# GQA attention fused with a squared-ReLU feed-forward: the third batch's loads get new end times in the kernel's event model, and scores wait per turned part

## The chip, the cores and the metric

The kernel runs on one core of a Trainium2 chip. The metric is the device time of one execution in microseconds (us); the figure for a kernel is the median of its runs. The engines are named as in the profile: PE is TensorE (PEld its weight loads), DVE is VectorE, ACT is ScalarE, POOL is GpSimd, SP is the sync engine, which here only issues DMAs.

## The reference, cut to what matters

```python
# q (8, 16, 384, 64), k and v (8, 4, 384, 64); each k/v head serves 4 q heads
scores = 0.125 * q @ k.T              # per head, 384 x 384
attn = softmax(scores)                # over the last axis
x = (attn @ v) -> (3072, 1024)        # batch and sequence by heads and head_dim
h = maximum(x @ w_in, 0)              # w_in (1024, 2048)
out = (h * h) @ w_out                 # w_out (2048, 1024), out (3072, 1024) float32
```

There are 8 batches of 384 tokens. A batch has 8 pairs of heads; pairs are numbered through, p = 0 to 63, so pair 16 is the first of batch 2, the third batch.

## The kernel before, in words

**Who does what.** For each pair, PE computes transposed scores from qT and kT (L514), ACT exponentiates them (L519), PE multiplies with v (L534), and DVE divides by the row sums into o_sb (L542, L544). The result is turned into xT, the feed-forward's input: by a DMA transpose on SP (put_x, L434), or for batch 1 by PE (row_turn, L571) and a DVE copy (L575). The feed-forward of a batch has 16 up tiles (row_up, PE L625): DVE applies the ReLU into one of three hr buffers (L636) and ACT squares hr into h2T (L644); for batch 0 every second tile is squared by POOL instead (L641). The down projection of batch 0 and of a part of batch 1 is plain (row_down, L683); the others take seven products for eight (L791), with sums made by DVE (L699).

**How inputs of a batch arrive.** POOL issues the loads of k, q and v (load_k L208, load_q L220, load_v L214), which also cast to bf16. There is one buffer of each for all batches from 1 on (k_st, q_next, v_st). POOL then copies k twice into k_dup (dup_all_k, L355), SP issues six DMA transposes (PARTS: two of k, L361, four of q, L369), and POOL copies v into v_aug (prepare_v, L383). load_third issues the loads of batch 2 and the second half of w_out behind them, as soon as the turns of batch 1 have freed q_next. The loads of later batches are issued by load_next when the second pair of the batch before them has been put.

**What sets the order.** A planner in Python writes out each engine's instructions in one fixed order. `Recorder.add` keeps a clock of its own: each operation gets a start and an end from the ends of what it depends on and from estimated durations (for a load 0.9 us on the queue and 12 us, LOADS, to landing; for a DMA transpose 1.25 and 2.2 us). `at(time, fn)` puts an action at a time of that clock. On the chip the engines follow the order, and wait on semaphores for what is really late; so a wrong estimate doesn't break the result, but an instruction can stand at the head of its queue and hold what is behind it. The clock is set to START, 30.0 us, after a hand-written beginning.

The main loop at the end picks the next work of PE among attention steps and feed-forward tiles, whichever can begin first. Attention is paced: each feed-forward piece adds its time over PACE of the present batch to a credit, and an attention step is due when the credit reaches the step's share. An attention step may be chosen only when its condition holds. For row_scores that is, before the change:

```python
return [piece(i) for i in range(3)], over, lambda: before in exped and p // NPB in prepared
```

`prepared` holds batches; batch b enters it when its sixth part has been issued. For batch 2 the order of attention is: attend of pair 15, both halves of the scores of pair 16, then on. The row-wise pieces use half of PE's rows each, so two of them run beside each other.

ready_at(b) places the preparation of a batch: at the time when k, v and q have all landed by the clock, it issues the k copy, the first part and the v copy, and then a part every 1.3 us.

Of the kernel before, what the change touches and what calls it, by code (L numbers as in the profile page):

```python
# [136 lines left out]
def bass_gqa_attention__then__ffn_squared_relu_kernel(  # L137
# [66 lines left out]
    sc_flat = sc_ps.ap().rearrange("p b c -> p (b c)")  # L204


    def load_k(b, after=()):
        R.add("gpsimd", lambda g: g.dma_start(  # L208
            k_st.ap().rearrange("p g j d -> p g (j d)"),
            k[b].rearrange("g (p j) d -> p g (j d)", j=NJ)),  # L210
            writes=["k_st"], dma="k", after=after, ns=900.0, lat=LOADS)

    def load_v(b, after=()):
        R.add("gpsimd", lambda g: g.dma_start(  # L214
            v_st.ap().rearrange("p g j d -> p g (j d)"),
            v[b].rearrange("g (p j) d -> p g (j d)", j=NJ)),
            writes=["v_st"], dma="v", after=after, ns=900.0, lat=LOADS)

    def load_q(b, after=()):
        R.add("gpsimd", lambda g: g.dma_start(  # L220
            q_st[1], q[b].rearrange("h (p j) d -> p h (j d)", j=NJ)),
            writes=[("q_st", 1, c) for c in range(NPB)], dma="q", after=after, ns=900.0, lat=LOADS)

    NWB = 8
    WC = FF // NWB
# [151 lines left out]
    def prepare(b, parts=range(6)):  # L377
        for i in parts:
            turn, x = PARTS[i]
            turn(b, x)  # L380
# [64 lines left out]
    def now():  # L445
        return R.idle_at["tensor"]
# [55 lines left out]
        return free.pop(0)  # L502

    exped, scaled = set(), {NPB - 1}
    turned, usable, upped = {}, {0}, set()

    def row_scores(p, half):
        kt, qt, keys, k_keys = operands(p)

        def piece(i):  # L510
            u = 3 * half + i
            j, x = u // 2, u % 2
            rows = ROWS[x]
            return Piece(x, 162.5, lambda pe: pe.matmul(sc_ps[:, i, 0:S], kt[rows, j * 128:(j + 1) * 128], qt[rows, :]),  # L514
                         keys + k_keys[j:j + 1], [("sc", i)])

        def over(last):
            def exp():
                R.add("scalar", lambda e: e.activation(expT[p % NEX][:, 3 * half:3 * half + 3, :], sc_ps[:, 0:3, 0:S],  # L519
                                                       AF.Exp, scale=0.125), ns=1130.0,  # L520
                      reads=[("sc", i) for i in range(3)], writes=[("expT", p % NEX, 3 * half + i) for i in range(3)])
                exped.add((p, half))

            at(R.ops[last]["end"], exp)

        before = (p, 0) if half else (p - 1, 1)
        return [piece(i) for i in range(3)], over, lambda: before in exped and p // NPB in prepared

    def row_attend(p, then=None):
        b, g = p // NPB, (p % NPB) // 2  # L530

        def piece(r, f, j):
            rows = ROWS[r]
            return Piece(r, 33.0, lambda pe: pe.matmul(  # L534
                po_v[:, f % NJ, f // NJ, :], expT[p % NEX][rows, 2 * j + f % 2, f // 2 * 128:f // 2 * 128 + 128],
                v_aug[b % 2][rows, g * NJ + j, :], start=(r == 0 and f == 0 and j == 0), stop=(r == 1),
                skip_group_check=True),
                [("expT", p % NEX, 2 * j + f % 2), ("v_aug", b % 2), ("v_one", b % 2)], ["po"])

        def done():  # L540
            rinv_v = rinv[p % 2].ap().unsqueeze(3)
            R.add("vector", lambda e: e.reciprocal(rinv_v, po_v[:, :, :, D:D + 1]),  # L542
                  reads=["po"], writes=[("rinv", p % 2)], ns=200.0)
            op = R.add("vector", lambda e: e.tensor_tensor(o_sb[p % NO][:, :, :, :], po_v[:, :, :, 0:D],  # L544
                                                           rinv_v.to_broadcast([128, NJ, 2, D]), ALU.mult),
                       reads=["po", ("rinv", p % 2)], writes=[("o_sb", p % NO, x) for x in range(2)], ns=560.0)
            scaled.add(p)
            assert b - NXT in upped or b < NXT
            if b == 1:
                at(R.ops[op]["end"], lambda: o_turns.append(p))  # L550
                return
            landed = put_x(p)
            turned[b] = turned.get(b, 0) + 1
            if turned[b] == NPB:
                usable.add(b)
            if then:
                then(landed)

        lo, hi = ([piece(r, f, j) for f in range(2 * NJ) for j in range(NJ)] for r in range(2))
        return lo, lambda last: hold_back(hi, last, done), lambda: p - 1 in scaled and ((p, 1) in exped)  # L560

    F_TURN = [sc_bf[:, 3, 0:S], sc_bf[:, 4, 0:S]] + [t.ap().bitcast(bf16)[:, 0:S] for t in f_ps]

# [18 lines left out]
    q_turns, o_turns = [], []  # L582

    def load_third():
        for load in (load_k, load_q, load_v):
            load(2)
        load_w_out(1)
        ready_at(2)

    def next_turn():  # L590
        if q_turns and (len(free) > 1 or not o_turns):
            c = q_turns.pop(0)

            def then():
                if c == NPB - 1:
                    prepared.add(1)
                    load_third()

            return row_turn(q_st[1][:, 2 * c:2 * c + 2, :].rearrange("p h e -> p (h e)"), [("q_st", 1, c)],
                            qT[1][:, c], [("qT", 1, c)], then)  # L600
        p = o_turns.pop(0)

        def then():
            turned[1] = turned.get(1, 0) + 1
            if turned[1] == NPB:
                usable.add(1)

        return row_turn(o_sb[p % NO].ap().rearrange("p i s d -> p (i s d)"), [("o_sb", p % NO, x) for x in range(2)],
                        xT[1][:, p % NPB], [("xT", 1, p % NPB)], then)
# [8 lines left out]
    def row_up(b, c, then=None, final=False):  # L618
        i = yield from next_bank()
        acc, key = F_BANKS[i]  # L620
        r = tiles[0] = (tiles[0] + 1) % NHR

        def piece(h, kc):
            rows = ROWS[h]
            return Piece(h, 162.5, lambda pe: pe.matmul(acc[:, 0:S], w_in_sb[rows, kc, c * 128:(c + 1) * 128],  # L625
                                                        xT[b % NXT][rows, kc, :], start=(h == 0 and kc == 0),
                                                        stop=(h == 1 and kc == NKC - 1), skip_group_check=True),
                         [("w_in", c * 128 // WC), ("xT", b % NXT, kc)], [key])

        def done():  # L630
            if r in hr_open:
                at(now() + 100.0, done)
                return
            hr_open.add(r)
            free.append(i)
            op = R.add("vector", lambda e: e.tensor_scalar_max(hr[r][:, :], acc[:, 0:S], 0.0),  # L636
                       reads=[key], writes=[("hr", r)], ns=560.0)

            def square():
                if b == 0 and c % 2:  # L640
                    op = R.add("gpsimd", lambda e: e.tensor_tensor(h2T[b % 2][:, c, :], hr[r][:, :], hr[r][:, :], ALU.mult),  # L641
                               reads=[("hr", r)], writes=h2(b, c), ns=830.0)
                else:
                    op = R.add("scalar", lambda e: e.activation(h2T[b % 2][:, c, :], hr[r][:, :], AF.Square),  # L644
                               reads=[("hr", r)], writes=h2(b, c), ns=520.0)
                squared.add((b, c))
                hr_open.discard(r)
                if then:
                    at(R.ops[op]["end"], then)

            at(R.ops[op]["end"], square)
            if final:
                upped.add(b)

        lo, hi = ([piece(h, kc) for kc in range(NKC)] for h in range(2))
        yield from push("up", lo, hi, done)
# [346 lines left out]
            yield from wait(lambda: b in usable)  # L1003
            yield from feed_forward(b)

    PACE = {1: (2300.0, 2300.0), 2: (4300.0, 3500.0), 3: (4500.0, 3600.0), 4: (6300.0, 4400.0), 5: (5800.0, 3800.0), **{b: (5800.0, 3800.0) for b in range(6, B + 1)}}
    LONE = 6000.0

    turns = [lambda banks=RING, g=g: first_kT(g, 1, banks) for g in range(HKV)]
# [44 lines left out]
    up_step(0, 0, 6, 8)  # L1054
    q_turns.extend(range(NPB - len(turns), NPB))
    exped.update(((NPB, 0), (NPB, 1)))
    prepared = {1}

    for o in R.ops:
        if o["dma"] is None or o["end"] < START:  # L1060
# [5 lines left out]
    def ready_at(b):  # L1066

        def part(i):
            prepare(b, (i,))
            if i < 5:  # L1070
                at(now() + 1300.0, lambda: part(i + 1))
            else:
                prepared.add(b)

        def begin():
            dup_all_k(b, "gpsimd")
            part(0)
            prepare_v(b)

        t = max(R.ready("gpsimd", ["k_st", "v_st"], []), R.ready("sync", [("q_st", 1, 0)], []))  # L1080
        at(t, begin)

    def load_next(b):
        def then(landed):
# [108 lines left out]
```

## Time and profile before

| | us |
|---|---|
| median of 5 runs | 426.71 |
| lowest and highest | 426.28, 427.42 |
| the profiled execution | 426.28 |
| its span, first to last instruction | 424.5 |
| busy: PE, PEld | 409.0, 314.2 |
| busy: DVE, ACT, POOL | 216.9, 215.0, 55.4 |
| mean granted PE clock | 0.992 |

How to read what follows. The page cuts the span into 40 slices of 10.6 us; a digit is the busy share in tenths, and PEclk is the clock that PE was granted. A window row gives for a stretch (from:to in us from the span's start) its length and, for PE, PEld, DVE, ACT and POOL in this order, the busy time and the instructions in brackets, then the granted clock, the share of the DMA engines' time and GB/s. A row of waits says which engine, at which line, waited for what: us in total, times, longest. A timeline row gives start, duration, engine, line, operation, what is written and read, and in square brackets the idle time before it and its releaser. A row of DMA queues has packets, MB, and the time that packets took as a share of 16 engines.

### The profile page before, as it was taken

How to read it: one execution, taken by the hardware profiler on the slowest of the kernel's cores; microseconds unless marked ns; L12 is line 12 of the kernel's file. 1: busy time of each engine (PE TensorE's matmuls, PEld its weight loads, DVE VectorE, ACT ScalarE, POOL GpSimd, SP SyncE). 2: the span in 40 equal slices, each digit the busy share in tenths (PEclk: the TensorE clock that was granted, in tenths of full speed). 3: DMA queues.
4: the chain of work that ended last, by engine and by line, in shares of the span. 5: the costliest groups of instructions: out<-in, count | busy, mean ns of one | idle time of the engine just before them, and what ended most of it. 6: DMA issues, size and time to landing. Idle time of an engine off the chain costs nothing.

```text
span 424.5 us, 13452 instructions
## 1 busy us (share of the span) xinstructions
PE 409.0 (96%) x6129; PEld 314.2 (74%) x6129; DVE 216.9 (51%) x480; ACT 215.0 (51%) x280; POOL 55.4 (13%) x70
## 2 busy tenths in 40 slices
PE   7989975999999999999999999999999999999997
PEld 4557753788877788768877788787886788779774
DVE  2664622245885446534556446634655445435453
ACT  4876732667665545654665446664664413313200
POOL 5824230310020103000030003000000000000000
PEclk9999988999999999999999999999999999999999
DMA  8999999296249758563068945854002220020012
GB/s 232 196 197 204 199 198 132 27 171 104 54 90 169 137 158 105 78 110 101 11 76 160 131 137 55 107 94 139 20 13 93 72 93 2 2 77 25 25 76 100
DMA packets 93353, 44.26 MB, mean 104 GB/s; under 512 B 71664, under 2 KB 87280, under 8 KB 93296
## 3 DMA queue, kind: packets, MB, share of 16 engines
q0 software_dynamic: 34288, 16.65, 31.0%
q1 hardware_dynamic: 55968, 24.49, 26.1%
q10 hardware_dynamic: 3040, 2.26, 1.8%
q8 instruction: 48, 0.79, 0.8%
q14 instruction: 9, 0.07, 0.0%
HBM read 35.65 MB, written 12.58 MB: 114 GB/s over the span
## 4 chain that ended last, share of the span: by engine, by line
PE 85%; DMA 10%; DVE 3%; ACT 1%; issue 1%; ACTq 0%; POOL 0%; DVEq 0%
PE f_ps L625 16%; PE sc_ps L791 16%; PE sc_ps L625 15%; PE f_ps L791 15%; PE po L534 10%; PE sc_ps L514 5%; DMA q_next<-in_q_dram 5%; DMA qT<-q_next 3%; PE f_ps L683 2%; DMA w_late<-in_q_dram 1%; PE sc_ps L683 1%; PE po L416 1%; PE sc_ps L399 1%; ACT expT L405 1%; DVE a_late L699 1%
## 5 line engine op out<-in xcount | busy, mean ns | idle before, releaser
L625 PE MATMUL f_ps<-xT,w_in_sb 64*128 64x384 bf16 x1040 | 172.8, 325 | 0.0
L519 ACT ACTIVATE expT<-sc_ps 128x1152 bf16<-128x1152 f32 x110 | 124.1, 1128 | 89.4 <-PE sc_ps L514 51.3
L625 PE MATMUL sc_ps<-xT,w_in_sb 64*128 64x384 bf16 x992 | 165.6, 324 | 3.5 <-DVE hr L636 3.5
L625 PEld LDWEIGHTS f_ps<-xT,w_in_sb 64*128 64x128 f16 x1040 | 90.6, 94 | 15.5
L625 PEld LDWEIGHTS sc_ps<-xT,w_in_sb 64*128 64x128 f16 x992 | 86.8, 94 | 18.3 <-DVE hr L636 4.3
L644 ACT ACTIVATE h2T<-hr 128x384 bf16<-128x384 f32 x119 | 61.2, 521 | 72.7 <-DVE hr L636 72.4
L534 PEld LDWEIGHTS po<-v_aug,expT 64*128 64x128 bf16 x2016 | 79.2, 95 | 14.7 <-DVE o_sb L544 1.6
L534 PE MATMUL po<-v_aug,expT 64*128 64x65 bf16 x2016 | 85.7, 191 | 0.0
L514 PE MATMUL sc_ps<-qT,kT 64*128 64x384 bf16 x330 | 57.9, 325 | 4.7 <-DMA qT<-q_next 4.7
L791 PE MATMUL sc_ps<-w_out_sb,a_late 64*128 64x512 f16 x240 | 59.9, 376 | 0.0
L791 PE MATMUL f_ps<-w_out_sb,h2T 64*128 64x512 f16 x240 | 59.4, 376 | 0.3 <-DVE hr L636 0.3
L636 DVE TENSOR_SCALAR hr<-f_ps 128x384 f32<-128x384 f32 x65 | 36.0, 556 | 42.6 <-PE po L534 17.9
L791 PE MATMUL sc_ps<-w_late,h2T 64*128 64x512 f16 x224 | 56.2, 376 | 0.0
L636 DVE TENSOR_SCALAR hr<-sc_ps 128x384 f32<-128x384 f32 x62 | 34.3, 556 | 37.5 <-PE sc_ps L625 20.7
L699 DVE TENSOR_TENSOR y_sb<-sc_ps,y_sb 128x512 f32<-128x512 f32 (+1 forms) x31 | 21.2, 687 | 40.3 <-PE sc_ps L791 24.1
L514 PEld LDWEIGHTS sc_ps<-qT,kT 64*128 64x128 bf16 x330 | 24.9, 94 | 10.7 <-DMA qT<-q_next 4.9
L791 PE MATMUL f_ps<-w_late,h2T 64*128 64x512 f16 x128 | 32.3, 376 | 0.0
L544 DVE TENSOR_TENSOR o_sb<-po,rinv 128x384 bf16<-128x384 f32 x56 | 31.2, 558 | 1.9
L791 PE MATMUL f_ps<-w_late,a_late 64*128 64x512 f16 x128 | 31.6, 376 | 0.0
L791 PEld LDWEIGHTS sc_ps<-w_out_sb,a_late 64*128 64x128 bf16 x240 | 21.8, 94 | 5.6 <-DVE y_sb L699 0.2
L791 PEld LDWEIGHTS f_ps<-w_out_sb,h2T 64*128 64x128 bf16 x240 | 21.7, 94 | 5.8 <-DVE hr L636 0.7
L542 DVE RECIPROCAL rinv<-po 128x6 f32<-128x6 f32 x56 | 10.9, 194 | 28.1 <-PE f_ps L791 8.8
(104 smaller groups left out, 422.9 us busy)
## 6 DMA issues: line engine op xcount, KB each, us to landing
out_dram<-y_sb SPq DMA_DIRECT2D x47, 256.0 KB, 2.3
q_next<-in_q_dram POOLq DMA_DIRECT2D x7, 768.0 KB, 10.9
w_in_sb<-in_moe_w_in_dram POOLq DMA_DIRECT2D x8, 512.0 KB, 12.3
w_out_sb<-in_moe_w_out_dram POOLq DMA_DIRECT2D x2, 2048.0 KB, 30.7
k_st<-in_k_dram POOLq DMA_DIRECT2D x7, 192.0 KB, 4.2
v_st<-in_v_dram POOLq DMA_DIRECT2D x7, 192.0 KB, 11.2
w_late<-in_q_dram ACTq DMA_DIRECT2D x1, 768.0 KB, 8.9
xT<-o_sb SPq DMA_TRANSPOSE x48, 2.4
```

Source lines behind the costliest of these rows:

```text
L399: m = pe.matmul(sc_ps[:, 2 * u + x, 0:S], kt[rows, j * 128:(j + 1) * 128], qt[rows, :])
L514: return Piece(x, 162.5, lambda pe: pe.matmul(sc_ps[:, i, 0:S], kt[rows, j * 128:(j + 1) * 128], qt[rows, :]), keys + k_keys[j:j + 1], [(" ...
L519: R.add("scalar", lambda e: e.activation(expT[p % NEX][:, 3 * half:3 * half + 3, :], sc_ps[:, 0:3, 0:S], AF.Exp, scale=0.125), ns=1130.0, ...
L534: return Piece(r, 33.0, lambda pe: pe.matmul(po_v[:, f % NJ, f // NJ, :], expT[p % NEX][rows, 2 * j + f % 2, f // 2 * 128:f // 2 * 128 + 128],
L542: R.add("vector", lambda e: e.reciprocal(rinv_v, po_v[:, :, :, D:D + 1]), reads=["po"], writes=[("rinv", p % 2)], ns=200.0)
L544: op = R.add("vector", lambda e: e.tensor_tensor(o_sb[p % NO][:, :, :, :], po_v[:, :, :, 0:D], rinv_v.to_broadcast([128, NJ, 2, D]), ALU.m ...
L625: return Piece(h, 162.5, lambda pe: pe.matmul(acc[:, 0:S], w_in_sb[rows, kc, c * 128:(c + 1) * 128], xT[b % NXT][rows, kc, :], start=(h == ...
L636: op = R.add("vector", lambda e: e.tensor_scalar_max(hr[r][:, :], acc[:, 0:S], 0.0), reads=[key], writes=[("hr", r)], ns=560.0)
L644: op = R.add("scalar", lambda e: e.activation(h2T[b % 2][:, c, :], hr[r][:, :], AF.Square), reads=[("hr", r)], writes=h2(b, c), ns=520.0)
L683: return Piece(h, 216.0, lambda pe: pe.matmul(acc, h2T[b % 2][rows, c, i * 128:(i + 1) * 128], w_out_sb[rows, c, jj * 512:(jj + 1) * 512], ...
L699: return R.add("vector", lambda e: e.tensor_tensor(out_ap, a, b, op), reads=reads, writes=writes, ns=ns)
L791: return Piece(h, 216.0, lambda pe: pe.matmul(acc, lhs[rows], right[rows, c], start=(first and h == 0 and c == 0), stop=(h == 1 and c == N ...
```

## The change

The end of the three loads of batch 2 is given by hand instead of estimated; the k copy, the turns and the v copy each get their own time in ready_at; `prepared` holds pairs of batch and part, and scores of a pair ask for the part of k and the part of q that they read; attend asks for its batch in `voiced`; squares of tiles 13 and 15 of batch 0 go from POOL to ACT; and two entries of PACE differ. No load, turn, matmul or store is added or taken away.

```diff
-    def load_k(b, after=()):
+    def load_k(b, after=(), end=None):
...
-            writes=["k_st"], dma="k", after=after, ns=900.0, lat=LOADS)
+            writes=["k_st"], dma="k", after=after, ns=900.0, lat=LOADS, end=end)
...
(load_v and load_q likewise)
...
+    voiced = {1}
...
         before = (p, 0) if half else (p - 1, 1)
-        return [piece(i) for i in range(3)], over, lambda: before in exped and p // NPB in prepared
+        parts = {(p // NPB, x) for x in ((0, 3)[p % NPB // 4], (1, 2, 4, 5)[p % NPB // 2])}
+        return [piece(i) for i in range(3)], over, lambda: before in exped and parts <= prepared
...
-        return lo, lambda last: hold_back(hi, last, done), lambda: p - 1 in scaled and ((p, 1) in exped)
+        return lo, lambda last: hold_back(hi, last, done), lambda: p - 1 in scaled and (p, 1) in exped and b in voiced
...
     def load_third():
-        for load in (load_k, load_q, load_v):
-            load(2)
+        for load, landed in ((load_k, 52000.0), (load_q, 57000.0), (load_v, 58500.0)):
+            load(2, (), landed)
         load_w_out(1)
         ready_at(2)
...
-                    prepared.add(1)
+                    prepared.update((1, i) for i in range(6))
                     load_third()
...
-                if b == 0 and c % 2:
+                if b == 0 and c % 2 and c < NFC - 3:
                     op = R.add("gpsimd", lambda e: e.tensor_tensor(h2T[b % 2][:, c, :], hr[r][:, :], hr[r][:, :], ALU.mult),
...
-    PACE = {1: (2300.0, 2300.0), 2: (4300.0, 3500.0), 3: (4500.0, 3600.0), 4: (6300.0, 4400.0), 5: (5800.0, 3800.0), ...
+    PACE = {1: (2300.0, 2300.0), 2: (4300.0, 3500.0), 3: (5000.0, 3900.0), 4: (5800.0, 4000.0), 5: (5800.0, 3800.0), ...
...
-    prepared = {1}
+    prepared = {(1, 0), (1, 1), (1, 3), (1, 2)}
...
         def part(i):
             prepare(b, (i,))
+            prepared.add((b, i))
             if i < 5:
                 at(now() + 1300.0, lambda: part(i + 1))
-            else:
-                prepared.add(b)

         def begin():
             dup_all_k(b, "gpsimd")
-            part(0)
-            prepare_v(b)
-
-        t = max(R.ready("gpsimd", ["k_st", "v_st"], []), R.ready("sync", [("q_st", 1, 0)], []))
-        at(t, begin)
+            at(max(now(), R.ready("sync", [("q_st", 1, 0)], [])), lambda: part(0))
+
+        at(R.ready("gpsimd", ["k_st"], []), begin)
+        at(R.ready("gpsimd", ["v_st"], []), lambda: (prepare_v(b), voiced.add(b)))
```

More of the change, by code (lines that the diff above doesn't have):

```diff
@@ L210, in load_k, with load_v @@
             k[b].rearrange("g (p j) d -> p g (j d)", j=NJ)),
-            writes=["k_st"], dma="k", after=after, ns=900.0, lat=LOADS)
-    def load_v(b, after=()):
+            writes=["k_st"], dma="k", after=after, ns=900.0, lat=LOADS, end=end)
+    def load_v(b, after=(), end=None):
         R.add("gpsimd", lambda g: g.dma_start(
@@ L216, in load_v, with load_q @@
             v[b].rearrange("g (p j) d -> p g (j d)", j=NJ)),
-            writes=["v_st"], dma="v", after=after, ns=900.0, lat=LOADS)
-    def load_q(b, after=()):
+            writes=["v_st"], dma="v", after=after, ns=900.0, lat=LOADS, end=end)
+    def load_q(b, after=(), end=None):
         R.add("gpsimd", lambda g: g.dma_start(
             q_st[1], q[b].rearrange("h (p j) d -> p h (j d)", j=NJ)),
-            writes=[("q_st", 1, c) for c in range(NPB)], dma="q", after=after, ns=900.0, lat=LOADS)
+            writes=[("q_st", 1, c) for c in range(NPB)], dma="q", after=after, ns=900.0, lat=LOADS, end=end)
     NWB = 8
@@ L1004, in all_feed_forward @@
             yield from feed_forward(b)
-    PACE = {1: (2300.0, 2300.0), 2: (4300.0, 3500.0), 3: (4500.0, 3600.0), 4: (6300.0, 4400.0), 5: (5800.0, 3800.0), **{b: (5800.0, 3800.0) for b in range(6, B + 1)}}
+    PACE = {1: (2300.0, 2300.0), 2: (4300.0, 3500.0), 3: (5000.0, 3900.0), 4: (5800.0, 4000.0), 5: (5800.0, 3800.0), **{b: (5800.0, 3800.0) for b in range(6, B + 1)}}
     LONE = 6000.0
```

## The prediction

> **What bounds the kernel now.** I read the page's slices first, then the windows around the one place where TensorE (PE) is not busy, then the waits there, then the queues that feed it.
>
> ```profile
> PE   7989975999999999999999999999999999999997
> PEclk9999988999999999999999999999999999999999
> ```
> ```profile
> 54.00:56.00 2.00, 1.46 (x35) 0.94 (x29) 0.00 (x0) 1.13 (x1) 0.00 (x0) 1.00 1.30 207
> 56.00:58.00 2.00, 0.00 (x0) 0.00 (x0) 0.16 (x1) 0.00 (x0) 1.88 (x3) 1.00 1.22 198
> 58.00:60.00 2.00, 1.54 (x25) 1.07 (x27) 1.63 (x5) 1.29 (x2) 0.52 (x1) 0.73 1.21 195
> 60.00:62.00 2.00, 2.00 (x22) 1.84 (x20) 0.26 (x1) 0.36 (x1) 0.83 (x1) 0.50 1.23 196
> 62.00:64.00 2.00, 2.00 (x43) 1.90 (x41) 1.02 (x3) 1.31 (x2) 0.00 (x0) 0.92 1.21 196
> 64.00:66.00 2.00, 1.17 (x28) 0.68 (x23) 1.11 (x3) 0.23 (x1) 0.64 (x1) 1.00 1.67 152
> 66.00:68.00 2.00, 0.00 (x0) 0.00 (x0) 0.00 (x0) 0.00 (x0) 0.18 (x1) 1.00 1.07 148
> 68.00:70.00 2.00, 0.15 (x2) 0.14 (x4) 0.00 (x0) 0.00 (x0) 0.00 (x0) 0.79 1.28 113
> ```
> PE is full from 75 us to the end (in 10 us windows it misses 0.55 us in 160 to 170 and 0.34 us in 270 to 280). It has two holes before: from 55.46 to 58.45 and from 65.08 to 69.85. After each the granted clock is 0.50 for a while. The clock column tells how long: 1.08 us of the window from 58, 2.0 us of the next and 0.32 us of the third at half speed, 3.4 us, so 1.7 us lost. The waits between 55 and 75 us name both holes:
>
> ```profile
> DVE hr L636 <- POOL h2T L641: 4.9, 1, 4.9
> POOL v_aug L383 <- DMA v_st<-in_v_dram: 3.6, 1, 3.6
> PE sc_ps L514 <- DMA qT<-q_next: 4.7, 1, 4.7
> PE sc_ps L625 <- DVE hr L636: 3.0, 1, 3.0
> ```
> Read from the last line up. First hole: PE's up-projection waits for a bank that VectorE (DVE) empties at L636; that waits for an hr buffer that GpSimd (POOL) squares at L641; and POOL stands at L383 for v of batch 2. Second hole: the first scores of batch 2 (pair 16) wait for the first DMA turn of q. The timelines of POOL and of SP's queue:
>
> ```profile
> 51.05 1.46 POOL L355 COPY k_dup<-k_st 128x1536 bf16<-128x1536 bf16 x1 [4.63 <-DMA k_st<-in_k_dram]
> 56.12 0.83 POOL L383 COPY v_aug<-v_st 128x768 bf16<-128x768 bf16 x1 [3.61 <-DMA v_st<-in_v_dram]
> 56.91 1.61 POOL L641 TENSOR_TENSOR h2T<-hr 128x384 bf16<-128x384 f32 x2
> ```
> ```profile
> 52.54 1.30 SPq L361 DMA_TRANSPOSE kT<-k_dup  x1
> 55.07 7.28 SPq L369 DMA_TRANSPOSE qT<-q_next  x2
> 62.38 4.23 SPq L361 DMA_TRANSPOSE kT<-k_dup  x1
> ```
> So k lands at 51.05, q at 55.07, v at 56.1. The first q turn is issued at 55.07 and the chain of waits has it for 14.73 us, to 69.80. The DMA view from 58 to 62 us shows why it is slow:
>
> ```profile
> q0 software_dynamic: 616, 0.63, 92.4%
> q1 hardware_dynamic: 618, 0.15, 29.5%
> ```
> q0 carries the second half of w_out (issued at 36.12, 33.7 us to landing: 69.8), q1 the turns. They take turns packet by packet, and the turn ends when w_out does.
>
> **The change, part by part.** The kernel's plan has its own clock; an "end" or "at" of the diff is on it. The first scores after START stand at 30.16 of the plan and at 31.49 of the trace: the trace is 1.3 us behind there.
>
> *End times of the third loads (52.0, 57.0, 58.5).* No load is issued at another time, so k, q and v land as now. Only the places of the dependent steps in each queue move. POOL's squares run 3.75 us apart (38.08, 41.82, 45.59), so the next, held up now, would come at 49.3, 53.1 and 56.8. The k copy is due at 52.06 of the plan, 53.4 to 54.1 of the trace: behind two squares, ending at about 55.4 instead of 52.51. The v copy is due at 58.56, behind the third square, at about 57.7, when v (56.1) is there. POOL then waits for no load, hr buffers come free, and the first hole goes: 2.99 us and the 1.7 us of half clock behind it, 4.7 us of PE time. Nothing else is late there: DVE's L636 takes 0.56 us, and the buffers are back before the next tile.
>
> *What is late next.* The second hole ends at 69.8, whatever PE does before. PE reaches it at 65.08 now and would, without the first hole, at 65.08 - 2.99 - 1.70 = 60.4. So removing the first hole alone brings nothing: the 4.7 us would be waited at the second. What counts is how much work the new plan puts ahead of the scores of pair 16.
>
> *Where these scores are placed.* row_scores may start once parts 0 and 1 are issued (57.06 and 58.36 of the plan) and their data are there by the plan: the q turn starts at 57.06 and is given 1.25 + 2.2 us, so 60.51, with the semaphore 60.57. In the plan of before (the start times that add works out for its own queue of operations) they stand at 58.32; the trace, undisturbed, at 60.4, is 2.1 us behind there. So 60.57 - 58.32 = 2.25 us more feed-forward work goes ahead of them (up tile 15 and row_down of batch 0, whose first w_out half landed at 22.23 + 27.8 = 50.0, fill it). With the 1.3 us lag at START instead of 2.1, the place is 61.9 of the trace and the work 1.5 us: 1.5 to 2.25; I take 2.2, since the lag of 2.1 is read at the spot. The loads are placed near their true landings, the turn is not: it is given 3.45 us (1.25 + 2.2), which is what turns of batch 3 take between 100 and 106 us (median 3.3), and not the 14.7 us that it takes beside w_out. PE reaches the wait at about 62.6 and stands there to 69.8, 7.2 us in one hole instead of 3.0 + 4.8 in two. The half clock after it is the same as after the second hole now.
>
> *Does the turn land later?* The k copy is 2.9 us later, so its turn goes at 55.5 (now 52.54) and the q turn at about 56.8 (now 55.07). Bounds: the turn slips by the whole 2.9 us, to 72.7; or w_out, shared with turns for 3 us less, ends earlier and the turn with it, in the nearest row at 67, when q0's share has fallen. I take no shift: on the engine that ends last, w_out and the first two turns are the same packets, served in another order, and their end is the same 69.8.
> [...]
>
> *The clock.* A hole of 2.99 us was followed by 3.4 us at 0.50. [...]
>
> *Squares 13 and 15 on ScalarE (ACT):* two of 0.52 us on an engine that is busy 2.96 of the 6 us from 58 on, for 0.83 us on POOL: nothing, or 0.3 us gained per tile where row_down waits for square 15; if ACT were full, 1.0 us lost. I take 0. *prepared and voiced:* conditions of the plan, not instructions; the other four turns landed at 70.4 to 72.1, and pair 18 comes some 7 us after pair 16. *Later batches:* begin no longer waits for v, so k copy and turns enter their queues about 1 us earlier in the plan; the six v waits of POOL (42.4 us) hold nothing but POOL. *PACE:* batch 3's attention is spread about 10% wider, batch 4's 8 to 9% closer. PE is full in both, so work is moved and not removed. Bounds from the only rows of PE waiting there: the two small holes, 0.9 us together, gone or doubled; I take 0.
>
> *Sum.* The profiled execution took 426.28 us (span 424.5 and 1.8 around it), 0.43 below the median of 426.71. 426.28 - 2.2 = 424.1, plus 0.43: **424.5**. Its own range: 1.5 instead of 2.2, and 0.9 either way: 423.6 to 426.1.
>
> **The rivals.** (1) *The turn lands earlier*, at about 67, because w_out is disturbed less. For it: from 66.6 us on q0's share falls to 57.8%. Against: w_out's last packets land at 69.8. It gives 2.8 us more: 421.7. (2) *Slower: the k copy behind two squares delays all turns.* SP's queue is in order, so the q turn stands behind the k turn, which waits for the copy. For it: the first k turn took 10.1 us and the q turn ended 7.2 us after it, so a chain that starts 2.9 us later may end 2.9 us later, at 72.7. Against: packets saved from turns go to w_out. It decides from a landing at 72.0 on (69.8 + 2.2); the price is 2.9 - 2.2 = 0.7: 427.4. (3) *No change:* the 2.2 us come, and the new order after 75 us gives them back in holes like those at 167 and 272 us (0.55 and 0.34); four more make 1.8: 426.3.
>
> **How the numbers follow.** Main case 0.56, (1) 0.13, (2) 0.17, (3) 0.14. About 0.2%, 0.85 us, is what a measurement of this kernel can tell. Faster: the main case but its upper edge, 0.53, and (1): 0.66. Same: (3), 0.14. Slower: (2) and the 0.03 of the edge where a small hole adds to it: 0.20. The range goes down to (1) and up to (2), with some of each left out: 421.3 to 427.4.
>
> **What the profile after would show.** Right: no wait of POOL at L383 with squares behind it, the k copy at 54 to 55.5 behind two squares, PE full from 33 to about 62.6, one hole to 69.8 for the q turn with about 7 us, half clock after it, full PE then. Wrong: a q turn that lands before 68 or after 71; a hole that is under 5 us, which says that more work went ahead than 2.2 us; or PE waits after 75 us that sum to over 2 us.

## The result, and the profile after

The changed kernel takes 425.06 us (median of 31 runs, 422.2 to 426.1) against 426.73 for the kernel before, measured beside it (52 runs, 425.1 to 428.64). The ratio is 0.9955, 95% interval 0.9944 to 0.9966: 1.9 us less, 1.5 to 2.4 (the two medians are 1.7 apart). The forecast was 424.5, 2.2 us less.

The profiled execution of the changed kernel took 422.44 us; only 2 of the 31 runs are faster, so its trace isn't typical. I show it first, and then the trace of a second profiled execution of the same kernel (424.54 us), which is nearer to the median. PE and its clock in the first, from the page, and its two windows from 33 to 40 us:

```profile
PE   8989997999999999999999999999999999999997
PEclk9996999999999999999999999999999999999999
```
```profile
33.00:36.00 3.00, 2.92 (x32) 2.14 (x34) 0.91 (x4) 0.71 (x1) 1.22 (x2) 0.51 1.47 202
36.00:40.00 4.00, 4.00 (x42) 2.42 (x38) 0.75 (x2) 1.13 (x1) 1.85 (x2) 0.51 1.33 200
```
The slice with 5 has become 7, and the first of two low slices is gone. But the clock is at half from 33 to 40 us, where before it was full, and full after the hole. That is 6.8 us at half speed, 3.4 us lost. PE comes that much later to the scores of pair 16, at 65.91, and so has less to wait there: 2.64 us, until 68.55.

The second trace, its waits of PE and its windows from 60 us on:

```profile
PE sc_ps L515 <- DMA qT<-q_next: 6.6, 1, 6.6
```
```profile
60.00:62.00 2.00, 2.00 (x52) 1.66 (x48) 1.07 (x2) 0.68 (x2) 0.00 (x0) 1.00 1.22 200
62.00:64.00 2.00, 0.85 (x9) 0.27 (x4) 1.02 (x3) 0.36 (x1) 0.00 (x0) 1.00 1.44 116
64.00:66.00 2.00, 0.00 (x0) 0.00 (x0) 0.00 (x0) 0.00 (x0) 0.00 (x0) 1.00 1.24 194
66.00:68.00 2.00, 0.00 (x0) 0.00 (x0) 0.00 (x0) 0.00 (x0) 0.00 (x0) 0.56 1.39 153
68.00:70.00 2.00, 0.53 (x4) 0.28 (x5) 0.00 (x0) 0.00 (x0) 0.00 (x0) 0.50 1.34 169
70.00:72.00 2.00, 2.00 (x18) 1.41 (x17) 0.00 (x0) 1.13 (x1) 0.00 (x0) 0.50 1.70 198
72.00:74.00 2.00, 2.00 (x17) 1.22 (x13) 0.36 (x1) 0.35 (x1) 0.00 (x0) 0.74 0.18 34
```
PE is full to 62.85 and stands to 69.47 (6.62 us). The half clock begins inside the hole, at about 66.2, and lasts to about 73. Of the four waits shown before, three are gone; the one for the turn is 6.6 us long instead of 4.7. The queues of POOL and SP in this trace:

```profile
53.16 0.83 POOL L643 TENSOR_TENSOR h2T<-hr 128x384 bf16<-128x384 f32 x1 [2.91 <-DVE hr L638]
53.93 1.46 POOL L355 COPY k_dup<-k_st 128x1536 bf16<-128x1536 bf16 x1
56.90 0.83 POOL L643 TENSOR_TENSOR h2T<-hr 128x384 bf16<-128x384 f32 x1 [1.51 <-DVE hr L638]
57.67 0.83 POOL L383 COPY v_aug<-v_st 128x768 bf16<-128x768 bf16 x1
```
```profile
55.42 1.30 SPq L361 DMA_TRANSPOSE kT<-k_dup  x1
56.78 8.46 SPq L369 DMA_TRANSPOSE qT<-q_next  x2
```
POOL waits for no load any more: the k copy and the v copy have no idle time before them. The turns are issued 2.9 and 1.7 us later than before, and the scores that read the first q turn start 0.4 us earlier, at 69.47 instead of 69.85.

### The profile page after: what moved, and what is told of

It reads as the page before. It is cut to its first block, busy times and chain, and to the rows that moved or that the text cites. A ratio compares the mean times of both kernels' runs of the same rounds, so it can differ in the third digit from the quotient of the medians.

```text
span 420.6 us, 13451 instructions
## 1 busy us (share of the span) xinstructions
PE 411.3 (98%) x6129; PEld 317.1 (75%) x6129; DVE 216.1 (51%) x480; ACT 216.7 (52%) x282; POOL 53.7 (13%) x68
## 4 chain that ended last, share of the span: by engine, by line
PE 91%; DMA 4%; DVE 3%; POOL 1%; ACTq 0%; issue 0%; SPq 0%; ACT 0%; DVEq 0%
PE f_ps L627 18%; PE sc_ps L627 18%; PE sc_ps L793 16%; PE f_ps L793 15%; PE po L536 12%; PE sc_ps L515 7%; DMA qT<-q_next 2%; PE sc_ps L685 2%; DMA w_late<-in_q_dram 2%; PE f_ps L685 1%; PE po L416 1%; PE sc_ps L399 1%; DVE o_sb L429 1%; PE sc_ps L330 0%; PE f_ps L330 0%; PE sc_ps L780 0%
## 5 line engine op out<-in xcount | busy, mean ns | idle before, releaser
L627 PE MATMUL sc_ps<-xT,w_in_sb 64*128 64x384 bf16 x992 | 168.6, 325 | 0.0
L646 ACT ACTIVATE h2T<-hr 128x384 bf16<-128x384 f32 x121 | 62.6, 520 | 69.2 <-DVE hr L638 68.3
L627 PEld LDWEIGHTS sc_ps<-xT,w_in_sb 64*128 64x128 f16 x992 | 87.9, 94 | 13.0 <-issue 0.2
L536 PE MATMUL po<-v_aug,expT 64*128 64x65 bf16 x2016 | 86.8, 191 | 0.0
L544 DVE RECIPROCAL rinv<-po 128x6 f32<-128x6 f32 x56 | 10.9, 195 | 33.6 <-PE f_ps L627 9.7
## 6 DMA issues: line engine op xcount, KB each, us to landing
v_st<-in_v_dram POOLq DMA_DIRECT2D x7, 192.0 KB, 10.9
```

The costliest lines, as they stand in the source:

```text
L536: return Piece(r, 33.0, lambda pe: pe.matmul(po_v[:, f % NJ, f // NJ, :], expT[p % NEX][rows, 2 * j + f % 2, f // 2 * 128:f // 2 * 128 + 128],
```

## The experiments

Theory A is the forecast's: the two holes are in series, the second ends when the q turn lands, at a time that the DMA engines set, and the gain is the work that stands ahead of the scores of pair 16. Rival B: the gain is made by the freed hr buffers, or by the pace. Where a time of the kernel before is given below, it was measured beside the run on the same chip; where none is given, that of the run above it holds. "Measured" gives the median, then the lowest and highest run, and the ratio with its 95% interval.

**The changed kernel once more** (no edit).

> The changed kernel once more, for a second trace and a fresh comparison. Theory A (the gain is the work that the plan puts ahead of the first scores of batch 2, 2.2 us, and the hole before them stays, ended by the DMA turn): median 424.3 to 425.3, a PE hole of 3 to 7 us that ends at 68 to 70, and half clock for 3.4 us either after it or at another place. Rival B (the first trace is the rule: the hole is 2.6 us, and no half clock follows): a hole under 3.5 us again and a time near 422.5.

Measured: 424.85 us (422.96 to 425.65), before 426.77, ratio 0.995 (0.9933 to 0.9968). This is the second trace above: A's hole, not B's. The half clock is longer than A had it, 6.8 us and not 3.4, but only 3.6 us of it lie behind the hole.

**The scores 3 us and 7 us later in PE's order.** One number each. The loads and the turns of batch 2 keep their order among themselves, but the rest of the plan moves with the scores: on SP's queue some stores and turns of xT change places, and with 64.0 two stores come between the turns of batch 2 (at 72.55 and 75.58 us).

```diff
-        for load, landed in ((load_k, 52000.0), (load_q, 57000.0), (load_v, 58500.0)):
+        for load, landed in ((load_k, 52000.0), (load_q, 60000.0), (load_v, 58500.0)):
```


> The changed kernel with one number changed: the plan's end of the q load of batch 2 is 60.0 instead of 57.0, so the scores of pair 16 stand 3 us later in PE's order; every load and turn is issued as before. Theory A: 3 us more work ahead of the same wait, so the hole is 3 us shorter: 421.5 to 422.5. Rival B (the gain came from the freed hr buffers and from the pace, and the place of the scores doesn't matter): 424.5 to 425.5, the hole moved and not shortened.

Measured: 420.28 us (418.86 to 421.47), ratio 0.9846 (0.9826 to 0.9866). The hole:

```profile
PE sc_ps L515 <- DMA qT<-q_next: 3.7, 1, 3.7
```
It is 2.9 us shorter, as A says, and ends at 69.09. But the time is 4.6 us less than the changed kernel's, 1.6 more than 3, and under A's range: its direction came, its size was missed. In the two profiled executions the spans differ by 422.7 - 419.0 = 3.7 us. The hole gives 3.3 of that (2.9 shorter, and over 0.4 us earlier). The half clock behind it lasts longer (5.0 us and not 3.6) and takes back 0.7. The last 1.1 us is busy time of PE: without what the half clock costs, it is busy 406.4 us instead of 407.5. The order of the work behind the scores is another too; why it takes less isn't shown.

```diff
-        for load, landed in ((load_k, 52000.0), (load_q, 57000.0), (load_v, 58500.0)):
+        for load, landed in ((load_k, 52000.0), (load_q, 64000.0), (load_v, 58500.0)):
```


> The changed kernel with the plan's end of the q load of batch 2 at 64.0 instead of 57.0: the scores of pair 16 stand 7 us later in PE's order, at about 69.6 of the trace, where the turn has landed. Theory A: no hole and no half clock in this stretch, 416 to 419. Rival B: 424 to 426. Rival C (the feed-forward has not enough work to fill 7 us more, since the second half of the down projection of batch 0 waits for square 15): part of the hole stays as PE waits for h2T, 419 to 422.

Measured: 417.14 us (414.69 to 419.74), ratio 0.977 (0.9738 to 0.9802). PE waits nowhere between 50 and 80 us in its trace. Neither B nor C: the feed-forward fills the 7 us. A number in the plan, without a faster instruction or an earlier load, is worth 7.7 us more than the change; how much of it is the hole and how much the new order behind it was not taken apart.

**The load of the second half of w_out behind the last turn**, in the changed kernel:

```diff
-            writes=[("w_out", i)], dma=f"wo{i}", end=(50500.0, 66500.0)[i])
+            writes=[("w_out", i)], dma=f"wo{i}", end=(50500.0, 80000.0)[i])
...
     def load_third():
...
-        load_w_out(1)
         ready_at(2)
...
             if i < 5:
                 at(now() + 1300.0, lambda: part(i + 1))
+            elif b == 2:
+                load_w_out(1)
```


> The changed kernel with the load of the second half of w_out issued behind the last turn of batch 2 instead of behind the loads of batch 2 (its planned end 80.0 instead of 66.5; it is first read after 100 us). Scores stand where the change puts them. Theory A with its cause of the late turn (the DMA engines alternate between w_out and the turns): the first q turn lands 3 to 5 us after its issue, at 61 to 64, PE has no hole of over 1 us at the scores of pair 16, and the time is 416 to 419. Rival D (turns of this batch are slow by themselves, or wait for q): the turn lands at 66 or later and the time is 423 to 425.

Measured: 416.2 us (415.1 to 419.77), ratio 0.9767 (0.9739 to 0.9795). PE doesn't wait at these scores. The DMA view from 60 to 61 us has the first q turn, issued at 60.65:

```profile
qT<-q_next SPq DMA_TRANSPOSE x1, 3.9
```
It takes 3.9 us from issue to landing instead of 14.7. (It lands at 64.5, a little later than forecast. This execution, 419.77 us, is the slowest of the six: its mean granted clock was 0.992, and every window from 55 to 415 us is at 1.00. So, as an estimate, some 6.7 us of its 418.0 were at half clock before 55 us, which put everything back.)

**The same in the kernel before**, where the first hole stays (load_w_out(1) moved from load_third to where the sixth part has been issued, with the same planned end of 80.0):

> The kernel before with the load of the second half of w_out issued behind the last turn of batch 2, the rest as before. Theory A: the first q turn lands 3 to 5 us after its issue at 55, so the second hole and its half clock go (4.8 and about 1.4 us), the first stays: 419.8 to 421.5. Rival D (something else holds the turn): 425 to 427.

Measured: 419.52 us (418.91 to 420.22), before 426.5, ratio 0.9841 (0.9817 to 0.9865). The DMA view of its stretch from 55 to 58 us, to be read against the 618 packets in 4 us and the 14.7 us of before:

```profile
q1 hardware_dynamic: 1884, 0.47, 83.4%
qT<-q_next SPq DMA_TRANSPOSE x2, 2.8
```
Without w_out beside them the turns get 1884 packets through in 3 us and land 2.8 us after issue. So it was w_out that held them, and rival D falls. The time is 0.3 us under A's range: 7.0 us gained, where the second hole and its half clock were priced at 6.2; what gives the rest is open. PE still waits for DVE's hr, and the first hole (3.0 us) now counts:

```profile
PE sc_ps L624 <- DVE hr L635: 3.5, 2, 3.0
```

**The first hole alone taken away**, in the kernel before:

```diff
             part(0)
-            prepare_v(b)
+            if b != 2:
+                prepare_v(b)
...
         at(t, begin)
+        if b == 2:
+            at(58500.0, lambda: prepare_v(b))
```


> The kernel before with the v copy of batch 2 placed at 58.5 of the plan and nothing else: squares no longer stand behind the wait for v, so the first hole goes, and the scores of pair 16 stay at 58.3 of the plan. Theory A: the hole of 3 us comes back in front of the scores, which wait for a turn that lands at 69 to 70 as before: one hole of 8 to 9.5 us, 426.0 to 427.2. Rival B (freeing the hr buffers is the gain): 422 to 424.8.

Measured: 426.75 us (425.56 to 427.58), before 426.5, ratio 1.0008 (0.9994 to 1.0022). Its waits of PE:

```profile
PE sc_ps L514 <- DMA qT<-q_next: 9.8, 1, 9.8
PE sc_ps L625 <- DVE hr L636: 0.5, 1, 0.5
```
The wait for hr shrinks from 3.0 to 0.5 us, PE comes to the scores at 59.75 and stands there for 9.8 us, to 69.58. Shortening a wait of 3 us to 0.5, with no half clock after it any more, brought nothing. This is the plainest test of A against B.

**The parts of the change.** The new ends, places and conditions, with PACE and squares as before:

> The changed kernel with PACE as before and squares 13 and 15 back on GpSimd: the new end times, places and conditions alone. Theory A (the whole gain is the work put ahead of the scores of pair 16): 424.3 to 425.4, as the changed kernel. Rival B (pace and squares make the gain, or take a part of it away): over 426, or under 423.8.

Measured: 423.98 us (423.47 to 424.28), before 426.5, ratio 0.9944 (0.9925 to 0.9963). The whole gain of the change is in this part; the interval contains the changed kernel's ratio, though the median is 0.9 to 1.1 us lower than its medians. It lies 0.3 us under A's range and does not reach B's 423.8, so it decides for neither by the ranges; that ends, places and conditions make the gain stands, while they were not taken apart among themselves.

> The kernel before with the two new entries of PACE alone. Theory A: no hole moves, 426.2 to 427.4. Rival B: 425.5 or less if the pace gains something by itself, 427.6 or more if it costs and the change gains more than 2.2 us elsewhere.

Measured: 425.71 us (424.38 to 426.63), ratio 0.998 (0.9965 to 0.9996). Both holes are where they were (2.8 and 4.3 us), so A's "no hole moves" holds for them, but the time is 0.8 us less, under A's range and just above B's 425.5: I had expected none. The two windows with the small holes of before:

```profile
160.00:170.00 10.00, 10.00 (x157) 7.45 (x153) 6.20 (x14) 6.34 (x11) 4.11 (x4) 1.00 0.65 76
270.00:280.00 10.00, 10.00 (x167) 7.55 (x164) 6.10 (x16) 6.38 (x10) 0.80 (x1) 1.00 0.60 66
```
The 0.55 and 0.34 us are gone, 0.9 together: that is the size of the gain, which is a match and not a test.

> The changed kernel with PACE as before; squares 13 and 15 stay on ScalarE. It tells which of the two makes the changed kernel about 1 us slower than the new ends alone (423.98). If PACE: 423.5 to 424.4. If the squares: 424.7 to 425.5. If the two only together, or if the difference is one of chip and moment: in between.

Measured: 424.27 us (423.0 to 425.64), before 426.48, ratio 0.9949 (0.9929 to 0.9969). That lies in the range that was set for PACE as the cause, 423.5 to 424.4. But its interval contains the ratios of the ends alone (0.9944) and of the changed kernel (0.995 and 0.9955), so whether either small part costs anything in the changed kernel stays open.

**A version that beats both:** the new ends, PACE and squares as before, and the late load of w_out.

> The new ends alone (PACE and squares as before) with the load of the second half of w_out behind the last turn of batch 2: both holes are attacked, each at its cause. Theory A: PE has no hole from 33 to 160 us; 415 to 417, as the changed kernel with the late load (416.2) or up to 1 us less. Rival: the pace was tuned for a run without holes and its old values cost here, 417.5 or more.

Measured: 414.5 us (414.2 to 418.08), before 426.48, ratio 0.9737 (0.9708 to 0.9766), 2.6% less and 0.5 us under A's range. From its windows:

```profile
50.00:60.00 10.00, 10.00 (x222) 7.83 (x218) 5.95 (x15) 6.77 (x8) 3.83 (x4) 1.00 1.03 130
60.00:70.00 10.00, 10.00 (x149) 6.59 (x145) 3.24 (x8) 5.05 (x5) 2.81 (x3) 1.00 1.04 142
70.00:80.00 10.00, 10.00 (x178) 8.50 (x176) 3.18 (x7) 7.21 (x9) 1.22 (x2) 1.00 1.29 183
```
PE is full and at full clock where the two holes were. Old and new prices agree: 4.8 and 3.0 us of holes and 3.1 us of half clock in the trace of before (1.7 us lost after the first hole, 1.35 of its 2.7 after the second) make 10.9 us, the small holes, which are gone too, 0.9 more, and 12.0 were gained.

## Why the prediction was right

*Both holes and what releases them:* right. The v copy has no wait and the squares stand where the working put them: squares at 53.16 and 56.90 (forecast 53.1 and 56.8), k copy at 53.93 (53.9), v copy at 57.67 (57.7).

*Removing the first hole alone brings nothing:* shown, 1.0008 (the kernel before with the v copy moved).

*Work put ahead, 2.2 us:* right. PE comes to the wait at 62.85 in the second trace; the forecast was 62.6. In the first it comes at 65.91, and 3.4 us of that are the half clock at 33 to 40: 62.5. So the hole of 2.64 us there, which the forecast had named as a sign of more work put ahead (under 5 us), came from the early half clock and not from more work.

*The turn doesn't land later although it is issued later:* right. The scores start at 69.47, 69.38, 69.15, 69.58 and 69.09 in the second trace and those of the ends alone, the pace alone, the first hole alone and the q end of 60, and at 69.85 before, for q turns issued between 54.77 and 56.92. In the second trace q0 had 670 packets and q1 400 between 58 and 62 us, where before it had been 616 and 618 (in that trace the two counts differ by 2 at most in each us from 57 to 65, 148 to 160 each): what the later turns leave, w_out takes. "The turn ends when w_out does" holds roughly: by the DMA views w_out and the first q turn land at 69.8 and 69.8 before, and at 67.5 and 68.6 in the first trace, whose q turn was issued last (59.85); in the second the turn lands at 69.4. So rival (2), the delayed k copy, falls. Rival (1), a turn that lands at 67, falls too; the first trace, with 68.55, comes nearest to it.

*The half clock after the hole, taken as the same:* a little too small. After 69.47 it lasts 0.53 + 2.0 + 1.04 = 3.6 us and costs 1.8; before, it lasted 2.7 us behind the second hole and cost 1.35. With the term: 2.25 of work, plus 0.38 for the earlier scores, less 0.45, is 2.2; the two spans differ by 424.5 - 422.7 = 1.8.

*PACE and the order after 75 us, taken as 0 within 0.9:* here the sum was lucky. PACE has an effect of its own in the order of before, 0.8 us (ratio 0.998), where the small holes that I used as its bound are gone. They are gone in the second trace too, but also in the three versions with the new ends and the old PACE (the ends alone, the old PACE with the new squares, the last version), so PACE is not what removes them there. Counted in, their 0.9 us make the sum 3.1 against 1.8. The other side stands on the page of the second trace:

```profile
PE 409.3 (97%) x6129; PEld 315.0 (75%) x6129; DVE 216.1 (51%) x480; ACT 216.6 (51%) x282; POOL 53.6 (13%) x68
```
PE was busy 409.0 us before. Without what the half clock cost while PE was busy (1.8 us here, 1.7 + 1.35 before) that is 407.5 us against 405.95: the same 6129 matmuls take some 1.5 us more in the new order (roughly, since the profile models the ends of matmuls). The forecast's sum had put both terms at nothing, and they nearly cancel. Why the new order takes longer isn't shown. With the new ends and the old PACE the same figure is 406.7 to 407.0, so PACE may have a part in it. Rival (3) falls as it was put, with new holes after 75 us: the second trace has no waits of PE after 80 us, the first a single one of 0.3 us. What the new order gives back, it gives back as busy time.

*Squares 13 and 15, taken as 0:* no difference is seen. With them on ACT and the old PACE the ratio is 0.9949, with them on POOL 0.9944, and the interval of each contains the other's ratio.

## What to carry to other kernels

When two waits of an in-order engine follow one another and the second ends at a time that the engine doesn't set, removing the first only lengthens the second (here from 4.7 to 9.8 us, with a ratio of 1.0008); price such a change by the work that comes to stand ahead of the second wait. In a planned order, a landing time for the load is not enough: what the engine reads is the turn, and its time beside a bulk load was 14.7 us (8.7 and 12.6 in the two traces after) and not 2.8 to 3.9. The transfer that makes the wait may have a reader far away, and then it is the thing to move: here the second half of w_out landed at 69.8 and was first read at about 108 us.

## What the runs showed of the hardware

These stretches at half clock were measured, each 3.4 us long or about two or three times that: 3.4 us after the 3.0 us hole of before, 3.4 around the end of its 4.7 us hole, 6.8 around the 6.6 us hole of the changed kernel, and 10.2 around the 9.8 us hole of the first-hole experiment (by its windows, 62 to 76). The clock also went to half without a large hole. From 30 to 33 us PE is busy 2.30 of 3.00 us in the trace of before and 2.29 in the first trace after, with small gaps (the longest 0.55 us); the first kept its clock (1.00 from 33 to 40 us), the second ran at half for 6.8 us (0.51 there). The trace of the q end of 64 shows such an early stretch too (2.21 us busy from 30 to 33, then 0.50 to 36 us and 0.54 to 40), and by its mean clock that of the late load in the changed kernel; that of the last version, with 2.21 us busy as well, stays at 1.00. The 2.6 us hole of the first trace after was followed by none (1.00 from 65 to 80 us). The 2.8 us hole of the pace alone was: a 64x384 matmul takes 0.32 us ahead of it and 0.52 behind it, as in the first trace after at 0.51. So holes of 2.8 and 3.0 us, and gaps of under 1 us each, were followed by half clock here, and one of 2.6 us was not; why one execution pays and another doesn't isn't shown.

Where no later wait takes it up, a stretch of 6.8 us costs about 3.4, an estimate from the clock of 0.51; in the first trace after, PE came 3.1 us later to the scores of pair 16 than in the second (65.91 against 62.85). The 3.4 us are about the distance of 418.08 from the other five runs of the best version (414.2 to 414.96): this run's mean granted clock is 0.991, theirs 1.0, and 0.9% of 416 us is 3.7; where in the run it lay isn't known.
